# One load of the keys into two alternating tiles, and the local scores of two heads on row tiles of 64 rows

## The chip, the core and the metric

The kernel runs on one core of one Trainium2 chip. The metric is the device time of one execution in microseconds. Three runs of the kernel before took 741.83, 742.13 and 745.91 us, so its median is 742.13 us.

## What is computed

Three layers follow each other: an attention with a coarse and a local part, a bilinear feed-forward layer, and a mixture of eight experts with the best one chosen for each token. Cut to what matters:

```python
# q, k, v: (4, 8, 576, 64): batch, heads, positions, head size
q_d, k_d, v_d = means of q, k, v over groups of 4 positions
out_up = repeat(softmax(q_d @ k_d.T / 8) @ v_d, 4)
mask = abs(pos[:, None] - pos[None, :]) < 4
out_local = softmax(where(mask, q @ k.T / 8, -1e9)) @ v
x = out_up + out_local                      # (2304, 512)
x = ((x @ w1) * (x @ w2)) @ w3 @ w_out      # moe_ weights, float64
e = argmax(x @ w_gate); gate from softmax and a sigmoid of x @ w_output_gate
out = gate * relu(x @ w1[e]) @ w2[e]        # 8 experts
```

The first-layer weights come as float64 and are turned into float32 by bit operations on VectorE; each is then split into a high and a low part, and a product is three matmuls (`mm3`, L397 to L400).

## The kernel before

The work of the attention is cut into 16 units, each two heads of one batch (so 128 rows: 64 of head 0 above 64 of head 1). A unit goes through five steps: `a_T` (L176) sums groups of four positions of the queries (on POOL, into `qz`) and of the keys (on DVE, L185, from `kc` into `kd`); `a_S1` (L188) makes the local scores and the coarse scores and their exponentials; `a_S2` (L220) normalises and sums the values in groups of four; `a_V1` (L239) transposes the weights; `a_V2` (L256) multiplies by the values and writes the sum into `xr`. The list `side` (L286 to L293) puts them in order: in a round come a_V2 of unit u-4, a_V1 of u-3, a_S2 of u-2, a_S1 of u-1 and a_T of u, and `step` (L295) takes one or two entries off that list at points between the other work.

That other work is, in order: the gate products (L315), the product of `w3` and `w_out` (`w3_part`, `wc_half`, L345 to L363), the conversion of `w1` and `w2` (`w_part`, L367), then six groups of 384 tokens (`g1_step`, `g2_step`), routing, and the experts. The first group needs the attention of its tokens in `xr` (`x_split`, L382).

Local scores: a query block of 32 positions (24 of them new) needs 32 keys. Twenty-four blocks make twenty-four float32 matmuls at L196, each on a column strip of 32 columns of the array (`tile_position=(0, 32 * j)`). The two heads are held apart by `kz`, a tile with two copies in its free dimension: rows 0 to 63 of copy 0 hold head 0's keys, rows 64 to 127 of copy 1 hold head 1's, and the rest is zero. A matmul with 128 rows and 2 x 32 columns thus gives both heads' scores side by side in one PSUM bank, and one addition at L200 puts on the mask. A float32 matmul that is written once shows as two records with a load of weights each.

Loads go through SP's queue. The keys are read twice per unit: whole into `kc` (L157, one buffer, for the sums of four) and in two halves into `kz` (L164, one buffer). The queries go into two alternating tiles `qT0` and `qT1` (L158). `a_load(u + 1)` follows a_T of u; `a_loadk(u + 1)` and the load of the coarse values `a_loadd(u)` (tile `v4`, "v" in the profile, L168) follow a_S1 of u.

PSUM has eight banks: two each for `g1` and `g2`, one for the bit operations, and three in `psa` (tag `at`), taken in turn: a new tile waits for the readers of the tile three turns earlier. A unit takes one for the local scores, one for the coarse scores, two in a_V1 and two in a_V2. Routing takes some as well.

The order on each engine is written by a scheduler from priorities and its own estimate of times; `burst()` (L149) raises the priority of a group of matmuls. Each engine then runs its list in order.

Of the kernel before, what the change touches and what calls it, by code (L numbers as in the profile page):

```python
# [8 lines left out]
F32 = mybir.dt.float32  # L9
# [6 lines left out]
ALU = mybir.AluOpType  # L16
AX = mybir.AxisListType
# [3 lines left out]
P = 128  # L21
B, H, S, D = 4, 8, 576, 64
# [6 lines left out]
NU = B * H // 2  # L29
# [19 lines left out]
def attention_moe_kernel(ctx: ExitStack, tc: tile.TileContext, q, k, vw_in, v4_in, w1, w2, w3, w_out,  # L49
                         w_gate, w_ogate, e_w1, e_w2, out):  # L50
    nc = tc.nc
# [5 lines left out]
    psa = actx.enter_context(tc.tile_pool(name="psa", bufs=3, space=PSUM))  # L57
# [7 lines left out]
    def mt(shape, dt, name, tag=None, bufs=None):  # L65
        return main.tile(shape, dt, name=name, tag=tag or name, bufs=bufs)
# [4 lines left out]
    mask = mt([P, 6, 32], F32, "mask")  # L71
# [36 lines left out]
    def f64_load(m, n):  # L108
        if m == "o":
            t = mt([P, 512], I64, "f64w", tag=f"W{n}")  # L110
            src = w_out[P * n:P * n + P, :]
        elif m == "3":
            t = mt([P, 512], I64, "f64w", tag=f"W{8 + n % 4}")
            src = w3[n]
        else:
            t = mt([P, 512], I64, "f64", tag=f"W{3 + 4 * m}") if n % 2 and n < 6 else mt([P, 512], I64, "f64", bufs=2)
            src = (w1, w2)[m][n]
        for c in pieces(m, n):
            nc.sync.dma_start(out=t[:, c], in_=src[:, c])
        staged[m, n] = t  # L120
# [17 lines left out]
    def at(shape, dt, name, bufs=1):  # L138
        return att.tile(shape, dt, name=name, tag=name, bufs=bufs)

    kz = at([P, 2, 584], F32, "kz")
    qTs = [at([P, 584], F32, f"qT{i}") for i in range(2)]
    bd = at([P, 12, 96], F32, "bd")
    qz = at([P, 2, 144], F32, "qz")
    for t in (kz, *qTs, bd, qz):
        nc.gpsimd.memset(t, 0.0)
    st = {}

    def burst():  # L149

        return tc.high_priority(offset=600)

    def a_load(u):
        d = st.setdefault(u, {})
        qT = qTs[u % 2]
        kc = at([P, S], F32, "kc")
        nc.sync.dma_start(out=kc, in_=k[u])  # L157
        nc.sync.dma_start(out=qT[:, 0:S], in_=q[u])  # L158
        d.update(kc=kc, qT=qT)

    def a_loadk(u):
        for h in range(2):
            c = slice(64 * h, 64 * h + 64)
            nc.sync.dma_start(out=kz[c, h, 3:3 + S], in_=k[u, c])  # L164

    def a_loadd(u):
        v4 = at([72, 2, 4, 2 * D], F32, "v4")
        nc.sync.dma_start(out=v4.rearrange("p k r n -> p (k r n)"), in_=v4_in[u])  # L168
        st[u]["v4"] = v4

    def a_loadv(u):
        vw = at([P, 6, 2 * D], F32, "vw")
        nc.sync.dma_start(out=vw.rearrange("p c n -> p (c n)"), in_=vw_in[u])
        st[u]["vw"] = vw

    def a_T(u):  # L176
        d = st[u]
        qv = d["qT"][:, 0:S].rearrange("p (n r) -> p n r", r=4)
        hs = at([P, 144, 2], F32, "pt")
        nc.gpsimd.tensor_tensor(hs, qv[:, :, 0:2], qv[:, :, 2:4], op=ALU.add)  # L180
        for h in range(2):
            c = slice(64 * h, 64 * h + 64)
            nc.gpsimd.tensor_tensor(qz[c, h], hs[c, :, 0], hs[c, :, 1], op=ALU.add)
        dn = at([P, 144], F32, "kd")
        nc.vector.tensor_reduce(out=dn, in_=d["kc"].rearrange("p (n t) -> p n t", t=4), axis=AX.X, op=ALU.add)  # L185
        d["kd"] = dn

    def a_S1(u):  # L188
        d = st[u]
        qT = d["qT"]  # L190
        ps = psa.tile([P, 512], F32, name="at", tag="at")
        sl = ps[:, 0:384].rearrange("p (b h k) -> p b h k", b=6, h=2)
        with burst():
            for g in range(24):
                b, j = divmod(g, 4)
                nc.tensor.matmul(sl[32 * j:32 * j + 32, b], qT[:, 24 * g:24 * g + 32], kz[:, :, 24 * g:24 * g + 32],  # L196
                                 start=True, stop=True, tile_position=(0, 32 * j))
        sm = at([P, 6, 2, 32], F32, "sm", bufs=2)
        mx = at([P, 6, 2], F32, "mx")
        nc.vector.tensor_tensor(sm, sl, mask.unsqueeze(2).to_broadcast([P, 6, 2, 32]), op=ALU.add)  # L200
        nc.vector.tensor_reduce(out=mx, in_=sm, axis=AX.X, op=ALU.max)
        nc.gpsimd.tensor_tensor(sm, sm, mx.unsqueeze(3).to_broadcast([P, 6, 2, 32]), op=ALU.subtract)
        ps = psa.tile([P, 512], F32, name="at", tag="at")
        sd = ps[0:96, 0:432].rearrange("p (q k) -> p q k", q=3)
        qf = qz.rearrange("p h n -> p (h n)")
        with burst():
            for qb in range(3):
                nc.tensor.matmul(sd[:, qb], qf[:, 96 * qb:96 * qb + 96], d["kd"], start=True, stop=True)  # L208
        ed = at([96, 3, 144], F32, "ed", bufs=2)
        md = at([96, 3], F32, "md")  # L210
        nc.vector.tensor_reduce(out=md, in_=sd, axis=AX.X, op=ALU.max)
        nc.vector.tensor_scalar(md, md, -1.0 / 128, None, op0=ALU.mult)
        zd = at([96, 3], F32, "zd", bufs=2)
        nc.scalar.activation(out=sm, in_=sm, func=AF.Exp, scale=0.125)
        for qb in range(3):
            nc.scalar.activation(out=ed[:, qb], in_=sd[:, qb], func=AF.Exp, scale=1.0 / 128,
                                 bias=md[:, qb:qb + 1], accum_out=zd[:, qb:qb + 1])
        d.update(sm=sm, ed=ed, zd=zd)
# [69 lines left out]
    for b in range(B):  # L288
        for s in range(UB + 4):
            for lag, fn in ((4, a_V2), (3, a_V1), (2, a_S2), (1, a_S1), (0, a_T)):  # L290
                if 0 <= s - lag < UB:
                    side.append((fn, b * UB + s - lag))
    side.reverse()  # L293

    def step(n=1):  # L295
        for _ in range(n):
            if side:
                fn, u = side.pop()
                with tc.high_priority(offset=120):
                    fn(u)  # L300
                if fn is a_V1:
                    a_loadv(u)
                if fn is a_T and u + 1 < NU:
                    a_load(u + 1)
                if fn is a_S1:
                    if u + 1 < NU:
                        a_loadk(u + 1)
                    a_loadd(u)


# [578 lines left out]
    for n in range(4):  # L889
        f64_load("3", n)  # L890
        if n == 1:
            a_load(0)
            a_loadk(0)
    gps = ps2.tile([P, 512], F32, name="g2", tag="g2")
    for f in range(KF):
        gate_step(f, gps, staged.pop(("o", f)))
        step(GSTEP[f])
# [16 lines left out]
    for i in range(KF):  # L914
        if i == KF - 2:
            ahead()
        w3T[i] = [mt([P, KF, P], F32R, "w3T", tag=f"W{12 + 2 * (i % 2) + z}") for z in range(2)]
        for hf in range(2):
            n = 2 * i + hf
            w3_part(i, hf, w3T[i], staged.pop(("3", n)), wf3)  # L920
            if n + 4 < 2 * KF:
                f64_load("3", n + 4)
            step(W3STEP[i][hf])
        if i < KF - 2:
            order = ((i, 0), (i, 1))
        else:
            order = ((KF - 2, 0),) if i == KF - 2 else ((KF - 1, 0), (KF - 2, 1), (KF - 1, 1))
        for n, hf in order:
            wps[n, hf] = wc_half(n, hf, w3T[n])
            if (n, hf) == (KF - 1, 0):  # L930
                wc_out(KF - 2, 0, wps.pop((KF - 2, 0)))
            if (n, hf) != (KF - 2, 0):
                wc_out(n, hf, wps.pop((n, hf)))
        step(W3STEP[i][2])
# [171 lines left out]
```

## Time and profile before

| | |
|---|---|
| median of three runs | 742.13 us |
| profiled execution | 743.41 us, its span 741.7 us |
| TensorE busy | 706.0 us (95%), mean granted clock 0.986 |
| DVE, POOL, ACT busy | 437.9, 324.5, 280.3 us |
| DMA | 97.72 MB, mean 132 GB/s |

An engine's busy time is the time in which one of its instructions ran; TensorE's matmuls overlap, so a busy TensorE is not always a full one. The span is the time from the first to the last instruction of the profiled execution. A wait is put down to what came last before the waiting instruction. SPq is the queue of SyncE that issues loads.

### The profile page before, as it was taken

To read this page: it belongs to the slowest core of one execution; us is meant where nothing else is said; L and a number is where in the kernel's file an instruction comes from. 1 tells how busy PE (TensorE), PEld (TensorE's weight loads), DVE (VectorE), ACT (ScalarE), POOL (GpSimd) and SP (SyncE) were. 2 spreads that over 40 slices of the span, in tenths; PEclk is the share of its full clock that TensorE was granted. 3 is DMA by queue.
4 is the path that set the end of the run, shared out by engine and by line. 5 is a ranking of instruction groups with operands and counts; after the bars stand their busy time and mean duration, and the time that the engine had idled before them with its cause. 6 is when DMAs were issued, how large, how long until landed. Compare 5 with 4: busy or idle time off the path is not lost.

```text
span 741.7 us, 14714 instructions
## 1 busy us (share of the span) xinstructions
PE 706.0 (95%) x5710; PEld 671.9 (91%) x5711; DVE 437.9 (59%) x940; ACT 280.3 (38%) x624; POOL 324.5 (44%) x306
## 2 busy tenths in 40 slices
PE   5788999999999999999999999989999999999995
PEld 3677889989989998998999999979999999999994
DVE  8979899872565437254342342575756756766730
ACT  3436356541254135034212221244454444544610
POOL 6845586950263146123012020155564755854611
PEclk9899999999999999999999999989999999999999
DMA  8998657611153133110100100566444645545301
GB/s 326 316 243 246 186 142 246 212 57 57 28 161 111 43 92 96 57 45 24 57 30 1 43 0 30 171 224 219 170 154 149 218 166 203 184 162 221 115 24 40
DMA packets 38265, 97.72 MB, mean 132 GB/s; under 512 B 6019, under 2 KB 12931, under 8 KB 38193
## 3 DMA queue, kind: packets, MB, share of 16 engines
q1 hardware_dynamic: 34768, 86.82, 36.4%
q0 software_dynamic: 3424, 9.93, 3.7%
q8 instruction: 46, 0.75, 0.4%
q14 instruction: 27, 0.21, 0.1%
HBM read 84.93 MB, written 12.29 MB: 131 GB/s over the span
## 4 chain that ended last, share of the span: by engine, by line
PE 76%; DMA 7%; POOL 6%; issue 6%; DVE 4%; ACT 1%; SPq 0%; POOLq 0%; DVEq 0%; ACTq 0%
PE g L398 22%; PE g L399 21%; PE g L400 21%; DMA v<-in_v_dram 3%; PE at L268 2%; DMA vw<-in_vw_dram 2%; PE at L208 1%; PE at L196 1%; PE tr L694 1%; PE at L264 1%; PE tr L787 1%; PE g L330 1%; PE at L252 1%; POOL out_dram L777 1%; DMA early<-in_moe_w_dram 1%
## 5 line engine op out<-in xcount | busy, mean ns | idle before, releaser
L398 PE MATMUL g<-xh,W 128*128 128x384 f32 x384 | 131.0, 341 | 0.6 <-DVE a L427 0.5
L400 PE MATMUL g<-xh,W 128*128 128x384 f32 x384 | 129.8, 338 | 0.7 <-POOL W L377 0.6
L399 PE MATMUL g<-xl,W 128*128 128x384 f32 x384 | 129.3, 337 | 0.0
L721 DVE TENSOR_TENSOR W<-raw,W 128x1024 fp32r<-128x1024 f32 x32 | 87.9, 2781 | 32.6 <-ACT W L719 23.5
L721 POOL TENSOR_TENSOR W<-raw,W 128x1024 fp32r<-128x1024 f32 x29 | 82.9, 2880 | 36.9 <-ACT W L719 36.9
L398 PE MATMUL g<-xT,W 128*128 128x288 f32 (+6 forms) x256 | 82.0, 320 | 1.0 <-ACT xT L698 1.0
L431 POOL TENSOR_TENSOR h<-a,h 128x384 fp32r<-128x384 f32 x30 | 30.8, 1028 | 118.4 <-ACT h L429 118.4
L399 PE MATMUL g<-xT,W 128*128 128x288 f32 (+6 forms) x256 | 80.1, 313 | 0.0
L400 PE MATMUL g<-xT,W 128*128 128x288 f32 (+6 forms) x256 | 79.8, 312 | 0.0
L398 PEld LDWEIGHTS g<-xh,W 128*128 128x128 f32 x384 | 72.2, 188 | 2.1 <-DVE a L427 0.9
L400 PEld LDWEIGHTS g<-xh,W 128*128 128x128 f32 x384 | 72.1, 188 | 2.0 <-POOL W L377 1.8
L399 PEld LDWEIGHTS g<-xl,W 128*128 128x128 f32 x384 | 72.2, 188 | 0.3 <-issue 0.2
L398 PE MATMUL g<-h,W 128*128 128x288 f32 (+5 forms) x224 | 69.9, 312 | 0.0
L399 PE MATMUL g<-wc,h 128*128 128x272 f32 (+1 forms) x240 | 68.2, 285 | 0.0
L398 PE MATMUL g<-wc,h 128*128 128x272 f32 (+1 forms) x240 | 68.2, 285 | 0.0
L399 PE MATMUL g<-h,W 128*128 128x288 f32 (+5 forms) x224 | 68.0, 303 | 0.0
L400 PE MATMUL g<-h,W 128*128 128x288 f32 (+5 forms) x224 | 68.0, 303 | 0.0
L400 PE MATMUL g<-wc,h 128*128 128x272 f32 (+1 forms) x240 | 67.8, 285 | 0.0
L719 ACT CAST W<-raw 128x1024 fp32r<-128x1024 f32 x61 | 60.0, 1046 | 8.3 <-DMA raw<-in_moe_w_dram 4.4
L427 DVE TENSOR_TENSOR a<-g,a 128x384 f32<-128x384 f32 x48 | 26.6, 554 | 61.9 <-PE g L400 49.6
L747 ACT ACTIVATE h<-g 128x288 fp32r<-128x288 f32 (+6 forms) x64 | 27.9, 437 | 78.1 <-PE g L400 74.2
L777 POOL DMA_INDIRECT out_dram<-orow,b_si x24 | 23.5, 978 | 62.9 <-DVE orow L776 59.3
(255 smaller groups left out, 1716.3 us busy)
## 6 DMA issues: line engine op xcount, KB each, us to landing
raw<-in_moe_w_dram SPq DMA_DIRECT2D x61, 512.0 KB, 3.5
f64w<-in_moe_w_dram SPq DMA_DIRECT2D x16, 512.0 KB, 8.5
f<-in_moe_w_dram SPq DMA_DIRECT2D x16, 512.0 KB, 4.7
vw<-in_vw_dram SPq DMA_DIRECT2D x16, 384.0 KB, 4.9
kc<-in_k_dram SPq DMA_DIRECT2D x16, 288.0 KB, 8.8
qT<-in_q_dram SPq DMA_DIRECT2D x16, 288.0 KB, 3.2
kz<-in_k_dram SPq DMA_DIRECT2D x32, 144.0 KB, 4.1
v<-in_v_dram SPq DMA_DIRECT2D x16, 288.0 KB
```

Of the source, the lines that this page charges most:

```text
L196: nc.tensor.matmul(sl[32 * j:32 * j + 32, b], qT[:, 24 * g:24 * g + 32], kz[:, :, 24 * g:24 * g + 32], start=True, stop=True, tile_positio ...
L208: nc.tensor.matmul(sd[:, qb], qf[:, 96 * qb:96 * qb + 96], d["kd"], start=True, stop=True)
L268: nc.tensor.matmul(xl[c // 3][64 * h:64 * h + 64, 96 * (c % 3):96 * (c % 3) + 96], vw[:, c, D * h:D * h + D], bd[:, 2 * c + h, :], start=T ...
L398: nc.tensor.matmul(ps, whi, xhi, start=first, stop=False)
L399: nc.tensor.matmul(ps, whi, xlo, start=False, stop=False)
L400: return nc.tensor.matmul(ps, wlo, xhi, start=False, stop=last)
L427: nc.vector.tensor_tensor(a, pp[1][:, 0:G], a, op=ALU.mult)
L431: eng.tensor_tensor(lo, a, hi.bitcast(F32), op=ALU.subtract)
L719: nc.scalar.copy(out=hi, in_=t)
L721: ins = eng.tensor_tensor(lo, t, hi.bitcast(F32), op=ALU.subtract)
L747: return nc.scalar.activation(out=t[:, 0, 0:C], in_=ps[:, 0:C], func=AF.Relu), nc.vector.scalar_tensor_tensor(t[:, 1, 0:C], ps[:, 0:C], 0. ...
L777: ins = nc.gpsimd.indirect_dma_start(out=out, out_offset=bass.IndirectOffsetOnAxis(ap=rt["si"][0:n, r, b:b + 1], axis=0), in_=t[0:n], in_o ...
```

## The change

The two-copy tile `kz` and the single tile `kc` go. Two tiles `kT0` and `kT1` take the keys of both heads as they come, by one load per unit, three positions in; the sums of four read from the same tile. The local scores are made by 48 written matmuls in place of 24: each takes the 64 rows of one head only (a row tile of 64 rows in the column strip of 32), with 32 columns, and each head has a PSUM bank of its own. Two mask additions with 192 columns each take the place of the one with 384. `a_loadk` and its calls go.

```diff
-    kz = at([P, 2, 584], F32, "kz")
+    kTs = [at([P, 584], F32, f"kT{i}") for i in range(2)]
...
-        qT = qTs[u % 2]
-        kc = at([P, S], F32, "kc")
-        nc.sync.dma_start(out=kc, in_=k[u])
+        qT, kT = qTs[u % 2], kTs[u % 2]
+        nc.sync.dma_start(out=kT[:, 3:3 + S], in_=k[u])
         nc.sync.dma_start(out=qT[:, 0:S], in_=q[u])
...
-    def a_loadk(u):
-        for h in range(2):
-            c = slice(64 * h, 64 * h + 64)
-            nc.sync.dma_start(out=kz[c, h, 3:3 + S], in_=k[u, c])
...
-        nc.vector.tensor_reduce(out=dn, in_=d["kc"].rearrange("p (n t) -> p n t", t=4), axis=AX.X, op=ALU.add)
+        nc.vector.tensor_reduce(out=dn, in_=d["kT"][:, 3:3 + S].rearrange("p (n t) -> p n t", t=4), axis=AX.X, op=ALU.add)
...
-        ps = psa.tile([P, 512], F32, name="at", tag="at")
-        sl = ps[:, 0:384].rearrange("p (b h k) -> p b h k", b=6, h=2)
+        sl = [psa.tile([P, 512], F32, name="at", tag="at")[:, 0:192].rearrange("p (b k) -> p b k", b=6) for _ in range(2)]
         with burst():
             for g in range(24):
                 b, j = divmod(g, 4)
-                nc.tensor.matmul(sl[32 * j:32 * j + 32, b], qT[:, 24 * g:24 * g + 32], kz[:, :, 24 * g:24 * g + 32],
-                                 start=True, stop=True, tile_position=(0, 32 * j))
+                for h in range(2):
+                    c = slice(64 * h, 64 * h + 64)
+                    nc.tensor.matmul(sl[h][32 * j:32 * j + 32, b], qT[c, 24 * g:24 * g + 32], kT[c, 24 * g:24 * g + 32],
+                                     start=True, stop=True, tile_position=(64 * h, 32 * j))
...
-        nc.vector.tensor_tensor(sm, sl, mask.unsqueeze(2).to_broadcast([P, 6, 2, 32]), op=ALU.add)
+        for h in range(2):
+            nc.vector.tensor_tensor(sm[:, :, h], sl[h], mask, op=ALU.add)
...
-                    if u + 1 < NU:
-                        a_loadk(u + 1)
                     a_loadd(u)
```

## Rows read from the trace of the kernel before

**Rows 1.** Stretches: start:end, length, each engine's busy us (instructions), clock, DMA share, GB/s.
```profile
18.50:37.00 18.50, 13.87 (x134) 11.89 (x135) 17.11 (x43) 7.98 (x19) 14.88 (x21) 0.85 1.04 314
...
0.00:111.00 111.00, 90.25 (x1000) 77.82 (x1002) 97.93 (x216) 49.51 (x131) 72.21 (x100) 0.95 0.81 243
111.00:350.00 239.00, 236.82 (x2090) 223.36 (x2089) 135.02 (x362) 91.23 (x245) 100.27 (x114) 1.00 0.31 96
```
**Rows 2.** Waits of TensorE, 111 to 360 us: us in total, times, longest.
```profile
PE at L208 <- POOL qz L183: 0.9, 1, 0.9
```
**Rows 3.** Waits of DVE, 0 to 111 us.
```profile
DVE kd L185 <- DMA kc<-in_k_dram: 3.8, 2, 2.4
DVE sT L243 <- POOL sm L228: 2.6, 1, 2.6
```
**Rows 4.** Line of time of DVE: start us, us, what [idle before, releaser].
```profile
44.36 0.75 DVE L185 TENSOR_REDUCE kd<-kc 128x144 f32<-128x576 f32 x1 [1.43 <-DMA kc<-in_k_dram]
...
55.24 0.75 DVE L185 TENSOR_REDUCE kd<-kc 128x144 f32<-128x576 f32 x1 [2.38 <-DMA kc<-in_k_dram]
```
**Rows 5.** Line of time of SP's queue, 26 to 47 us.
```profile
26.64 0.33 SPq L158 DMA_DIRECT2D qT<-in_q_dram  x1
...
35.91 0.33 SPq L157 DMA_DIRECT2D kc<-in_k_dram  x1
...
40.74 1.11 SPq L164 DMA_DIRECT2D kz<-in_k_dram  x2
41.91 0.58 SPq L158 DMA_DIRECT2D qT<-in_q_dram  x1
...
46.08 0.33 SPq L157 DMA_DIRECT2D kc<-in_k_dram  x1
```
**Rows 6.** Waits of POOL, 0 to 111 us.
```profile
POOL v L235 <- DMA v<-in_v_dram: 18.6, 6, 5.3
```
**Rows 7.** Groups of instructions by form, DVE, 0 to 360 us: busy us, mean ns.
```profile
L200 DVE TENSOR_TENSOR sm<-at,mask 128x384 f32<-128x384 f32 x16 | 8.7, 541 | 0.2
...
L279 DVE TENSOR_TENSOR xr<-at,up 128x192 f32<-128x192 f32 x8 | 2.8, 346 | 0.0
```
**Rows 8.** Line of time of TensorE at unit 4's local scores.
```profile
86.00 0.88 PE L196 MATMUL at<-kz,qT 128*32 128x64 f32 x48
86.81 0.38 PE L400 MATMUL g<-wo,w3T 128*128 128x256 f32 x1
```
**Rows 9.** The tile `at` on TensorE: duration of one, ns, least/median/most.
```profile
L196 PE MATMUL at<-kz,qT x768: 216/219/317, 22.4 to 340.1; 128*32 128x64 f32 x192
...
L208 PE MATMUL at<-kd,qz x96: 283/286/447, 24.5 to 339.3; 128*96 128x144 f32 x96
```
**Rows 10.** Line of time of TensorE, coarse scores of unit 0.
```profile
24.96 0.65 PE L208 MATMUL at<-kd,qz 128*96 128x144 f32 x4
```
**Rows 11.** Stretch of 35 ns, L196 alone: TensorE (starts), weight loads (starts), clock, DMA.
```profile
116.43:116.47 0.04, 0.03 (x4) 0.03 (x4) 1.00 0.28 117
```
**Rows 12.** Lines of time of ACT, DVE and TensorE around unit 7's scores.
```profile
116.38 0.69 ACT L253 COPY pt<-at 72x288 f32<-72x288 f32 x2 [0.67 <-PE at L252]
...
120.44 0.54 DVE L200 TENSOR_TENSOR sm<-at,mask 128x384 f32<-128x384 f32 x1
...
116.44 0.86 PE L196 MATMUL at<-kz,qT 128*32 128x64 f32 x44
...
118.92 0.67 PE L268 MATMUL at<-bd,vw 128*64 128x96 f32 x12
...
122.35 0.72 PE L268 MATMUL at<-bd,vw 128*64 128x96 f32 x12
```
**Rows 13.** Line of time of TensorE at unit 8's scores.
```profile
198.24 0.31 PE L196 MATMUL at<-kz,qT 128*32 128x64 f32 x6
198.48 0.49 PE L208 MATMUL at<-kd,qz 128*96 128x144 f32 x2
...
200.88 0.40 PE L581 MATMUL at<-rb 128*128 128x288 f32 x1
```

More of the change, by code (lines that the diff above doesn't have):

```diff
@@ L144, in attention_moe_kernel @@
     qz = at([P, 2, 144], F32, "qz")
-    for t in (kz, *qTs, bd, qz):
+    for t in (*qTs, *kTs, bd, qz):
         nc.gpsimd.memset(t, 0.0)
@@ L154, in a_load @@
         d = st.setdefault(u, {})
-        qT = qTs[u % 2]
-        kc = at([P, S], F32, "kc")
-        nc.sync.dma_start(out=kc, in_=k[u])
+        qT, kT = qTs[u % 2], kTs[u % 2]
+        nc.sync.dma_start(out=kT[:, 3:3 + S], in_=k[u])
         nc.sync.dma_start(out=qT[:, 0:S], in_=q[u])
-        d.update(kc=kc, qT=qT)
-    def a_loadk(u):
-        for h in range(2):
-            c = slice(64 * h, 64 * h + 64)
-            nc.sync.dma_start(out=kz[c, h, 3:3 + S], in_=k[u, c])
+        d.update(kT=kT, qT=qT)
     def a_loadd(u):
@@ L189, in a_S1 @@
         d = st[u]
-        qT = d["qT"]
-        ps = psa.tile([P, 512], F32, name="at", tag="at")
-        sl = ps[:, 0:384].rearrange("p (b h k) -> p b h k", b=6, h=2)
+        qT, kT = d["qT"], d["kT"]
+        sl = [psa.tile([P, 512], F32, name="at", tag="at")[:, 0:192].rearrange("p (b k) -> p b k", b=6) for _ in range(2)]
         with burst():
@@ L892, in attention_moe_kernel @@
             a_load(0)
-            a_loadk(0)
     gps = ps2.tile([P, 512], F32, name="g2", tag="g2")
```

## The prediction

> **What bounds the kernel now.** I read the stretches first, then who waits in each. From 111 to 350 us TensorE is busy 236.8 of 239 us at clock 1.00, while DVE has 135 and the DMA engines 0.31 [rows 1]; its waits there are of three kinds, the largest of them 0.9 us [rows 2]. So in that stretch every nanosecond of TensorE counts one for one. From 0 to 111 us it is another machine: TensorE has 90 of 111 us, DVE 98, and between 18 and 37 us the DMA engines read 1.04, that is full [rows 1]. The prologue (the float64 conversions, the product of w3 and w_out, and seven units' local scores) ends when DVE has done its list, so what counts there is DVE's work and DVE's idle time. The largest idle item is the reduction of the keys (L185) waiting for its load: 3.8 us in two waits; the next is 2.6 us [rows 3]. Both waits are seen on DVE's line of time, 1.43 us before 44.36 and 2.38 us before 55.24 [rows 4].
>
> **Loads.** The change removes 32 transfers of 144 KB (two a unit) and puts the one load of the keys, 288 KB, into two alternating tiles. What that is worth is read on SP's queue: the queries of unit 2 were asked for at 26.64, its keys only at 35.91, since the single kc tile had first to be reduced for unit 1; the queries of unit 3 at 41.91, its keys at 46.08 [rows 5]. The queries already alternate, and the new key tile has the same kind of wait: the readers of unit u-1, whose local scores come before a_T(u) in the order of steps. So the keys go out beside the queries, 9.3 and 4.2 us earlier; a landing took about 8.4 us (35.91 to 44.36) and 9.2 us (46.08 to 55.24) [rows 4, 5], so unit 2's keys land at about 35 and unit 3's at about 51, both before DVE's wait begins (42.9 and 52.9). Both waits go: **-3.8 us**. The bound on the other side is 0, if DVE finds another wait in that place. Late next is the value load: POOL stood 18.6 us in the prologue waiting for it [rows 6], and it reaches DVE only through the 2.6 us item. Queued behind the new load on SP are the queries, the weights and the values, as behind the old; the pair of kz issues held SP for 1.11 us a unit [rows 5], and that goes. Five pairs fall before 75 us, 1.5 MB; at the 314 GB/s of that stretch [rows 1] this is 4.7 us of a full DMA system. DVE's next wait is for POOL, not for a DMA [rows 3], so I take 0 and keep -4.7 as the bound. The first load now follows the memset of its tile, done on POOL long before the weights on SP let that load go: nothing.
>
> **DVE.** One mask addition over 384 columns (541 ns) becomes two of 192, each priced as L279 with 128x192, also out of PSUM: 346 ns [rows 7]. That is 2 x 346 - 541 = 151 ns a unit, **+1.1 us** for the seven units of the prologue. The nine later ones lie under TensorE; without that cover they cost +1.4. The reduction reads the same 576 columns, three further in: nothing.
>
> **TensorE.** Twenty-four products are written now, 48 records with a load of weights each; one unit's burst starts at 86.00 and the next work at 86.81, so 0.81 us [rows 8]. Its 48 starts lie within 0.88 - 0.22 = 0.66 us [rows 8, 9]; the four column strips run side by side, so that is 12 rounds of 55 ns, 0.86 ns for each of 64 columns. L208, on the whole array, agrees: (0.65 - 0.29)/3 = 0.121 us for 144 columns, 0.84 [rows 9, 10]. After the change there are 96 records with 32 columns on eight tiles (two row tiles, four strips). No row shows row tiles. Lower bound of the time: all eight run together, 12 rounds of about 29 ns, 0.35 us. Then the pace of starting matters: in 35 ns four pairs of load and matmul started [rows 11], the first at 116.44, so at most 8 ns a pair; 96 pairs at 8 ns are 0.77 us. Upper bound: nothing faster than the mean pace of today's burst, 0.66/48 = 14 ns, which is 1.32 us. A unit thus costs -0.31, +0.11 or +0.66 us. I take the first, because the four strips already run fully side by side and a strip's two row tiles write to different banks. In the bound stretch nine units (7 to 15) count: **-2.8 us**, with ends of -2.8 and +5.9. In the prologue TensorE is no bound: 0.
>
> A start every 14 ns on average [rows 8, 9] is faster than a rule of the Trainium skill allows (TensorE: Matmul & The Clock Gate, "Wait — 56ns, not 53.3ns?": start to start never falls below about 25 ns, however few columns). By that rule, as an estimate, 96 starts would take 2.4 us and the nine units would cost about +16 us; this trace contradicts it for work spread over strips.
>
> **PSUM.** The pool `psa` has three banks and each unit now takes seven turns of it instead of six; the local scores and the coarse scores of one unit need all three. A turn waits for the reader three turns back. The second head's bank now waits for the first copy of V1's transposes (before, only the coarse scores did), and the next V2 waits with its first bank for the mask addition (before, with its second). Behind a waiting matmul stands the whole of TensorE's order. For unit 7 the copies begin at 116.38 while the scores begin at 116.44 and a copy takes 0.35 [rows 12]: about 0.4 us. Five late units (7, 10, 11, 14, 15) come right after a V1, so 0 to 2.0; I take the middle, **+1.0 us**.
>
> **Sum.** The profiled execution took 743.4 us, 1.3 over the median of the runs shown, 742.1. 743.4 - 3.8 + 1.1 - 2.8 + 1.0 = 738.9, and 1.3 less for the median: **737.6**.
>
> **The rivals.**
> *The starts hold the burst at 8 ns.* For it: a pair of load and matmul has never been seen closer. Against: both run on tiles that were idle. -2.8 becomes +1.0: 741.4.
> *The prologue keeps its length.* The keys come early, but DVE then waits for the values' chain (POOL's 18.6 us). -3.8 becomes 0: 741.4.
> *Twice the matmuls at today's mean pace, 14 ns*, because row tiles of one strip take turns or starts cost more. -2.8 becomes +5.9: 746.3. The whole turns slower than before where a pair takes more than about 9 ns (0.66 us plus a ninth of the 1.7 that the rest gains, over 96). The eight starts in 35 ns speak against it.
> *The bank ring stalls TensorE (the slower side).* At unit 7, V2's first bank started at 118.92 and its second only at 122.35, after the mask addition that began at 120.44 and takes 0.54 [rows 12]. If now the first also waits to 120.98 and nothing is placed between, 2.1 us are lost at each of the five units: +10.5 in place of +1.0, 747.1. It decides from 1.1 us a unit on. Against: the scheduler put other matmuls between, and can again.
> *The bursts are torn.* At unit 8 the scores and the coarse scores alternate and take 198.24 to 200.88, 2.64 us [rows 13], where 0.81 and about 0.9 in one piece would do (six records of 0.121, and 0.15 for the change of shape, as 0.81 is over 0.66). Units 8, 9 and 15 look so. That the heads stand side by side then isn't true: if all nine are torn, 6 x 0.9 = +5.4: 743.0. If none is, -2.7.
>
> **How the numbers follow.** Forecast 0.44, pace of 8 ns 0.15, prologue keeps its length 0.15, pace of 14 ns 0.10, ring 0.10, torn 0.06. About 0.5% (3.7 us) is what a measurement of this kernel tells from no change, so faster means below 738.4 and slower above 745.8. Of the forecast nearly all lies below 738.4 (0.40), of the two at 741.4 a fifth (0.06): faster 0.46. The slower cases give 0.14 (the 14 ns pace lies on the line), the rest is 0.40. The low end takes the forecast, the DMA bytes in part and whole bursts (737.6 - 3.4 - 2.7), 731.5; the high end stops short of the two slower rivals, 745.5.
>
> **What would show it.** DVE has no wait for the keys in the prologue, and TensorE's full stretch begins about 3 us earlier; if not, the loads' step is wrong. The burst's 96 records span about 0.35 us and the next work starts 0.5 us after the first; 0.77 or 1.3 names the pace. The mask additions last 346 ns each. Waits of TensorE's local-score lines for ACT's copies or DVE's additions between 111 and 350 us, above 1 us in all, mean the ring. Most of all the prediction fails if the order that the scheduler writes differs elsewhere: a later x_split or more torn bursts would cover all these terms.

## The result: slower by 6.7 us, and the profile after

The changed kernel took 748.89 us (median), the kernel before 742.18 us in the same series: a ratio of 1.0075, 95% interval 1.0058 to 1.0092. The forecast of 737.6 us and its range, which ended at 745.5, were missed on the other side. The profiled execution took 750.43 us, its span 748.7 us (743.41 and 741.7 before).

Stretches of the changed kernel (start:end, length, busy us and instructions of PE, PEld, DVE, ACT, POOL, clock, DMA share, GB/s):

```profile
18.50:37.00 18.50, 15.81 (x285) 12.64 (x284) 16.63 (x32) 7.38 (x19) 13.82 (x19) 1.00 1.00 344
37.00:55.00 18.00, 14.16 (x185) 12.08 (x185) 15.76 (x47) 6.70 (x24) 11.88 (x16) 0.72 0.56 173
0.00:111.00 111.00, 90.83 (x1308) 77.94 (x1310) 101.52 (x220) 49.71 (x136) 68.66 (x98) 0.94 0.68 223
111.00:350.00 239.00, 233.93 (x2489) 222.47 (x2488) 141.80 (x368) 86.97 (x231) 101.12 (x114) 1.00 0.27 84
```

The kernel before, 37 to 55 us:

```profile
37.00:55.00 18.00, 15.70 (x198) 13.18 (x198) 14.02 (x32) 7.24 (x21) 8.20 (x9) 0.96 0.94 246
```

Set beside [rows 1], the loads did what they should: the DMA share of 37 to 55 us fell from 0.94 to 0.56, and by 111 us DVE had idled 9.5 us instead of 13.1. But DVE was busy 3.6 us more and got no further: it ran 220 instructions by then, 216 before, and 7 of the 220 are second mask additions. The additions account for 1.1 us; the rest is that the same instructions took longer. The eight subtractions of w3 on DVE, before and after (0 to 111 us; busy us, mean ns):

```profile
L351 DVE TENSOR_TENSOR w3T<-wf,w3T 128x512 fp32r<-128x512 f32 x8 | 7.6, 948 | 0.0
```

```profile
L346 DVE TENSOR_TENSOR w3T<-wf,w3T 128x512 fp32r<-128x512 f32 x8 | 10.1, 1257 | 0.2 <-ACT w3T L344 0.2
```

TensorE's clock in 37 to 55 us was 0.72, where it was 0.96; but the kernel before had its slow stretch sooner (0.85 in 18.5 to 37 us [rows 1], now 1.00), and over 0 to 111 us the clock is 0.94 against 0.95. The first matmul of the first group (`xh`) starts at 111.7 us instead of 105.2, the last of that group at 171.2 instead of 163.0, and from 365 us on everything is 6.6 to 7.2 us late. So the loss arises in the prologue and in the first group.

The keys on SP's queue in the changed kernel, for units 2 and 3, and the largest waits of DVE from 0 to 111 us (waited for: us in total, times, longest):

```profile
26.56 0.33 SPq L156 DMA_DIRECT2D kT<-in_k_dram  x1
...
33.87 0.33 SPq L156 DMA_DIRECT2D kT<-in_k_dram  x1
```

```profile
DVE md L208 <- PE at L205: 2.2, 1, 2.2
DVE xr L276 <- ACT up L268: 1.5, 2, 1.3
DVE su L222 <- ACT sm L211: 1.4, 1, 1.4
```

The keys are asked for 9.4 and 12.2 us sooner than in [rows 5]. The wait of [rows 3] for them is gone from DVE's list; other waits, for TensorE and ACT, stand there now.

What TensorE did from 29 to 44 us is read on its line of time (start us, us, what, [idle before, releaser]):

```profile
29.70 1.13 PE L192 MATMUL at<-kT,qT 64*32 64x32 f32 x72
30.76 0.98 PE L205 MATMUL at<-kd,qz 128*96 128x144 f32 x6
31.66 0.33 PE L192 MATMUL at<-kT,qT 64*32 64x32 f32 x24
31.92 1.06 PE L325 MATMUL g<-wot,wg 128*32 128x128 f32 x8
...
35.37 0.38 PE L333 MATMUL g<-ident,gs 128*128 128x128 f32 x2
36.96 0.70 PE L249 MATMUL at<-ident,ed 96*72 96x96 f32 x6 [1.09 <-DVE sm L197]
...
39.82 0.86 PE L192 MATMUL at<-kT,qT 64*32 64x32 f32 x48 [2.02 <-ACT ed L213]
...
41.78 0.59 PE L393 MATMUL g<-wo,w3T 128*128 128x272 f32 x1 [1.09 <-DVE wo L337]
42.92 0.59 PE L394 MATMUL g<-wo,w3T 128*128 128x272 f32 x1 [0.55 <-DVE wo L338]
43.31 0.43 PE L395 MATMUL g<-wo,w3T 128*128 128x272 f32 x1
```

Unit 1's keys were there early, so the scheduler put its scores (29.70) ahead of the last gate products (31.92) and of the gate's transposes (35.37). In the kernel before they came at 37.79, behind the gate's transposes at 28.36. Half of the w3 product multiplies by the gate's columns, which DVE copies out of those transposes. The eight copies, before and after (duration ns, first and last start us):

```profile
L342 DVE CAST wo<-g x8: 153/158/175, 28.8 to 37.7; 128x16 fp32r<-128x16 f32 x8
```

```profile
L337 DVE CAST wo<-g x8: 133/158/163, 41.6 to 54.2; 128x16 fp32r<-128x16 f32 x8
```

They come 13 to 16 us later, though the transposes come only 7.0 us later: DVE's list has conversions and attention steps ahead of the first copy. TensorE waits for the copies at 41.78 and 42.92. Two other waits in that line are of the bank ring: V1's transposes at 36.96 for a mask addition, unit 2's scores at 39.82 for ACT to have read a bank of coarse scores. From 38.4 to 48.6 us TensorE runs at a granted clock of 0.50, the lower of its two levels (1.2 of 2.4 GHz): a matmul with 272 columns takes 0.43 us at 43.31 (0.59 right behind a wait), where it takes 0.29 at the full clock. The kernel before has such a stretch too, from 31.6 to 38.4 us. How far the w3 product has come by 80 us (its matmuls alone: length, busy us and count, clock, DMA share, GB/s), before and after:

```profile
0.00:80.00 80.00, 28.73 (x182) 0.94 0.88 269
```

```profile
0.00:80.00 80.00, 27.25 (x158) 0.91 0.76 252
```

Up to the first matmul on `xh`, and from there to the end of the first group, before and after:

```profile
0.00:105.20 105.20, 84.71 (x941) 72.84 (x942) 92.13 (x201) 46.20 (x123) 66.41 (x94) 0.95 0.82 247
105.20:163.00 57.80, 56.29 (x473) 51.76 (x470) 49.28 (x99) 30.91 (x76) 46.06 (x47) 1.00 0.58 184
```

```profile
0.00:111.70 111.70, 91.53 (x1314) 78.64 (x1316) 102.22 (x221) 50.41 (x137) 69.36 (x98) 0.94 0.68 222
111.70:171.20 59.50, 54.45 (x482) 49.73 (x481) 48.40 (x87) 26.49 (x62) 43.46 (x44) 1.00 0.50 154
```

In the prologue TensorE thus idled no longer than before (20.2 us, 20.5 before). It lost 1.7 us more to the half clock there, and the local and coarse scores of units 0 to 6 held it 16.1 us instead of 13.3. The idle time that is new lies in the first group: 5.1 us instead of 1.5. The weights that this group multiplies by are converted 4.6 us later at the first (ACT's L371 at 108.2, 103.6 before) and 8.1 us later at the sixteenth (167.4, 159.3). The largest wait for them, with what it goes back to on DVE and POOL:

```profile
113.42 2.62 DVE L226 TENSOR_SCALAR zd<-zd 96x3 f32<-96x3 f32 x1
...
114.06 1.96 POOL L387 TENSOR_TENSOR xl<-xr,xh 128x384 fp32r<-128x384 f32 x2
...
115.96 0.67 DVE L129 SCALAR_TENSOR_TENSOR wf<-f,cv 128x512 uint32<-128x512 uint32 x1
...
116.66 0.62 ACT L371 CAST W<-wf 128x512 fp32r<-128x512 f32 x1 [3.54 <-DVE wf L129]
...
117.33 0.44 PE L393 MATMUL g<-xh,W 128*128 128x384 f32 x1 [2.18 <-ACT W L371]
```

The scaling of `zd` has 3 columns and took 0.17 us at the median before. Here it took 2.62 and ended 0.03 us after POOL's subtraction, and the conversion stood behind it.

### The profile page after: what moved, and what is told of

Same layout as the page of the kernel before. It is cut to its first block, busy times and chain, and to the rows that moved or that the text cites. A ratio compares the mean times of both kernels' runs of the same rounds, so it can differ in the third digit from the quotient of the medians.

```text
span 748.7 us, 16209 instructions
## 1 busy us (share of the span) xinstructions
PE 710.3 (95%) x6478; PEld 676.7 (90%) x6479; DVE 449.8 (60%) x956; ACT 279.5 (37%) x624; POOL 325.4 (43%) x307
## 4 chain that ended last, share of the span: by engine, by line
PE 77%; DVE 8%; issue 5%; POOL 4%; DMA 4%; ACT 1%; SPq 0%; POOLq 0%; DVEq 0%; ACTq 0%
PE g L393 22%; PE g L395 22%; PE g L394 22%; PE at L192 2%; PE at L205 2%; PE at L265 2%; DMA v<-in_v_dram 1%; PE tr L689 1%; PE at L261 1%; PE tr L782 1%; POOL W L372 1%; DVE cv L127 1%; PE g L325 1%; DMA early<-in_moe_w_dram 1%; DVE wf L129 1%
```

## The experiments

Theory A: the scheduler used the early keys to put attention ahead of the gate's finishing, and this place costs TensorE. Theory B: the row tiles themselves cost (twice the matmuls, seven turns in three banks, two additions). Theory C: every new order is a throw of the dice. The numbers are medians of five rounds; in brackets the ratio to the kernel before on the same chip (742.1 to 743.4 us) and its interval.

**Holding the early attention steps.** In the changed kernel, the steps of the first two rounds of w3 may follow only behind the gate's last transpose and last copy.

```diff
-            step(W3STEP[i][hf])
+            if i < 2:
+                with tc.issue_after(held[0]), tc.issue_after(held[1]):
+                    step(W3STEP[i][hf])
```

> The changed kernel with one thing put back: the first four attention steps that are traced after gate_finish (sums of unit 1, scores of unit 1 and so on) are queued on TensorE and DVE behind gate_finish's last transpose and its last copy. Loads, row tiles, banks and additions stay as in the changed kernel. Theory A (the keys come early, so the scheduler puts unit 1's scores and sums ahead of the finishing of the gate, and the product of w3 and w_out starts late): the w3 product is back within 1 us of the kernel before at its tenth part (42.8 us) and the time falls by 5 to 7 us, to 742 to 744. Theory B (row tiles: twice the matmuls, three banks a unit, two additions): the time stays within 2 us of the changed kernel's 748.9. Theory C (a lottery of the order, nothing in particular): anything between 742 and 750, with the loss in another stretch.

744.99 us, 1.0028 (1.0008 to 1.0048). That is 3.9 us under the changed kernel, where A had expected 5 to 7. By 80 us the w3 product had 240 matmuls done, where the changed kernel had 158 and the kernel before 182. From its tenth part on, its matmuls came 3 to 14 us earlier than in the kernel before. So the place of those steps does cost TensorE, as A says. The lead over the kernel before was all given back further on, line of TensorE and a stretch:

```profile
108.69 0.25 PE L192 MATMUL at<-kT,qT 64*32 64x32 f32 x4 [1.07 <-ACT pt L250]
...
111.35 0.74 PE L261 MATMUL at<-pt,vd 72*64 72x144 f32 x2 [0.72 <-DVE sm L197]
```

```profile
111.00:125.00 14.00, 13.65 (x84) 10.76 (x85) 8.17 (x20) 6.70 (x20) 8.26 (x10) 0.63 0.37 111
```

Two ring waits, then V2 and the scores by turns of two, and 14 us at a clock of 0.63.

**Row tiles alone, out of `kz`, with the loads of before.**

```diff
+                for h in range(2):
+                    c = slice(64 * h, 64 * h + 64)
+                    nc.tensor.matmul(sl[h][32 * j:32 * j + 32, b], qT[c, 24 * g:24 * g + 32], kz[c, h, 24 * g:24 * g + 32],
+                                     start=True, stop=True, tile_position=(64 * h, 32 * j))
```

> The kernel before with the row tiles alone: 48 written matmuls of 64 rows out of kz, a bank for each head, two mask additions; kc, kz and their loads as before. Theory A: the keys of unit 1 still come late, its scores stay behind the gate, and the time is within 2 us of before (741 to 744), with about 0.15 us more for each burst. Theory B: 747 to 750. Theory C: anything between.

747.27 us, 1.0075 (1.0046 to 1.0104). This is B's range: unit 1's scores (37.2 us) stand behind the gate's transposes (30.6) here, and the kernel is slower by 5.1 us all the same.

**A single key tile.** This kernel reads other data: the keys of unit u+1 are loaded before unit u's local scores are written, so those scores use the next unit's keys. It serves for its order alone.

```diff
-    kTs = [at([P, 584], F32, f"kT{i}") for i in range(2)]
+    kTs = [at([P, 584], F32, "kT0")]
```

> The changed kernel with one key tile in place of two: one load a unit, row tiles and banks as in the change, but a load must wait until the unit before has used the tile. Theory A: the keys are late again, the gate is finished before any scores of unit 0, the time is 741 to 745. Theory B: 747 to 750.

738.22 us, 0.9944 (0.9922 to 0.9967). Here every score waits for the following keys, and the gate is finished before any score. A later start of the attention was faster than both kernels.

**Early sums alone**: the kernel before with two alternating `kc` and the loads of `kz` as they were.

```diff
+    kcs = [at([P, S], F32, f"kc{i}") for i in range(2)]
...
-        kc = at([P, S], F32, "kc")
+        kc = kcs[u % 2]
```

> The kernel before with two alternating tiles kc for the sums of the keys, nothing else: this is the loads' term of the prediction by itself. Both of DVE's waits for the keys (3.8 us) should go. The prediction's step: 3.8 us less, 738 to 739. Theory A: the scores still wait for kz, so the gate stays ahead of unit 1's scores; DVE's waits go, but other work of DVE or TensorE is late next, 740 to 743. Theory B: 740 to 743.

749.67 us, 1.0093 (1.0062 to 1.0123). DVE's waits for keys are gone, unit 1's scores (38.8 us) stay behind the gate's transposes (28.7), and the kernel is slower by 7.5 us, outside the ranges of A and B. Both halves lose; B and C can't be told apart by them.

**Nearly the same order of scores with and without the change.** On TensorE the scores of units 1 to 6 are held behind the matmuls of the w3 product (counted as written) behind which they stood, or nearly stood, before. In both kernels the attention steps are also taken off `side` sooner (`W3STEP`; in the second table of holds `GSTEP` too). The second table of holds starts later, as the single tile did: {0: 31, 1: 72, 2: 119, 3: 184, 4: 312, 5: 368}.

```diff
-W3STEP = ((1, 1, 0), (1, 1, 0), (1, 1, 0), (1, 1, 0), (1, 1, 1), (1, 1, 1), (1, 1, 0), (1, 1, 0))
+W3STEP = ((1, 1, 1), (1, 1, 1), (1, 1, 1), (1, 1, 1), (1, 1, 1), (1, 0, 0), (1, 0, 0), (1, 0, 0))
+HOLD = {1: 25, 2: 72, 3: 112, 4: 224, 5: 261, 6: 324}
...
+                    if fn is a_S1 and u in HOLD:
+                        hold.enter_context(tc.issue_after(mml[HOLD[u] - 1]))
```

> The kernel before with a hold on TensorE only: the local and coarse scores of units 1 to 6 may not start before the 25th, 72nd, 112th, 224th, 261st and 324th matmul of the w3 product, the places that they have (or nearly have) in the kernel before. It is the control of the next run. Theory A (the place of the early scores against the gate's finishing decides): about the time of before, 740 to 745 us. Theory B (the row tiles cost, whatever the order): the same. Theory C (every new order is a throw of the dice): anything from 736 to 750.

> The changed kernel with the same hold as the run before it: unit 1's scores come after the gate's finishing again. Theory A: the loss of 6.8 us goes; the difference to the held kernel before is the sum of the small terms only (loads -3.8 to 0, additions +1.1, bursts at 8 ns a pair +0.1 a unit, ring 0 to 2), so -2 to +3 us, some 740 to 745. Theory B (twice the matmuls, three banks, two additions): +5 to +7 against the held kernel before, as row tiles alone gave +5.1, so 747 to 750. Theory C: no fixed relation to the run before it.

> The kernel before with later scores: unit 0's first scores after the 31st matmul of the w3 product (so behind the gate's finishing), those of units 1 to 5 after the 72nd, 119th, 184th, 312th and 368th: the order that the single key tile fell into (738.2 us). Theory A: finishing the gate first lets TensorE work earlier on the w3 product; faster than before by 2 to 6 us, 736 to 740. Theory B says nothing of it and keeps 742. Theory C: 736 to 750.

> The changed kernel with the later scores of the run before it. Theory A: faster than the changed kernel by 9 to 14 us and within -2 to +3 us of the held kernel before, 735 to 742. Theory B: 5 to 7 us over the run before it whatever that is. Theory C: no fixed relation.

| holds | before | changed | the change is worth |
|---|---|---|---|
| none | 742.18 | 748.89 | +6.7 |
| old places | 748.67 (1.0070, 1.0046 to 1.0093) | 738.79 (0.9955, 0.9932 to 0.9977) | -9.9 |
| later | 752.01 (1.0113, 1.0082 to 1.0144) | 739.10 (0.9947, 0.9924 to 0.9969) | -12.9 |

B falls as it stood: in two of three orders the changed kernel is the faster one, and in both it beats the kernel before without holds by 0.5%. A holds for the changed kernel: with unit 1's scores behind the gate again, and the other units held too, it gains 10.1 us. It doesn't hold as a rule, since a later start made the kernel before slower. And the control missed its expectation of 740 to 745 us: in the kernel before, the holds left the scores of units 1 to 3 behind the same 25, 72 and 112 matmuls and those of units 4 to 6 behind 12 more each, and it lost 6.5 us. So -9.9 and -12.9 compare two held kernels, of which the one before suffers from the holds; C is not refuted. Nor do the scores stand behind the same matmuls in both kernels of the first pair: those of units 1 to 4 start behind 25, 72, 112 and 224 in the kernel before and behind 15, 67, 126 and 248 in the changed one. Stretches 28 to 80 us of the changed kernel with the scores at their old places:

```profile
28.00:55.00 27.00, 23.76 (x359) 19.90 (x357) 26.63 (x73) 12.15 (x40) 18.86 (x24) 1.00 0.71 240
55.00:80.00 25.00, 25.00 (x320) 23.08 (x318) 22.79 (x48) 15.20 (x40) 12.03 (x12) 1.00 0.75 235
```

and of the kernel before with the same holds:

```profile
28.00:55.00 27.00, 20.81 (x208) 17.66 (x208) 22.88 (x60) 10.23 (x30) 14.78 (x18) 0.81 0.96 268
55.00:80.00 25.00, 22.60 (x252) 20.87 (x249) 20.09 (x45) 13.47 (x41) 15.17 (x18) 0.93 0.72 212
```

In the first DVE is idle for 0.4 of 27 us and TensorE's clock doesn't fall; in the second DVE idles 4.1 us with the DMA engines at 0.96, and the clock falls three times by 80 us. By 111 us DVE had run 235 instructions in the first, 206 in the second. This is the gain that the forecast hoped for; in the changed kernel without holds, with 220, it isn't there.

**Whole bursts.** One hold, the coarse scores of a unit behind its last local score on TensorE, keeps the two from alternating.

```diff
-        with burst():
+        with burst(), tc.issue_after(loc.ins):
             for qb in range(3):
                 nc.tensor.matmul(sd[:, qb], qf[:, 96 * qb:96 * qb + 96], d["kd"], start=True, stop=True)
```

> The kernel before, with one hold: the coarse scores of a unit come after its last local score on TensorE, so that the two no longer alternate. Theory T (torn bursts cost what the change of shape costs): local and coarse scores of 16 units took 17.1 + 15.1 us of TensorE's time before; whole they would take 16 x (0.81 + 0.9) = 27.4, so -2 to -5 us, 737 to 740. Theory A (the place of the early scores and TensorE's clock in the prologue decide): unit 0 and 1 stay where they were, so 742 with what T gives in the full stretch only, 739 to 742.

> The changed kernel with the same hold; unit 1's scores still stand ahead of the gate's finishing. Theory A: the loss of 6.8 us before 111 us stays, with a gain of 2 to 4 us from the full stretch: 745 to 748. Theory T (the loss of the change is its torn bursts): 741 to 743.

> The changed kernel with unit 1 to 6's scores held at their old places (738.8 us) and whole bursts besides. Theory T: local and coarse scores took 20.4 + 15.9 us in that run, whole about 27 to 30, so -3 to -8 us: 731 to 736. Theory A: no tearing counts where TensorE waits anyway; nine late units in the full stretch give -1 to -3: 736 to 738.

> The changed kernel with the later scores (739.1 us) and whole bursts. Theory T: -3 to -8 us, 731 to 736. Theory A: -1 to -3, 736 to 738. Either way under the kernel before.

Before 737.77 (0.9923, 0.9894 to 0.9953), changed 749.57 (1.0094, 1.0058 to 1.0129), changed with old places 748.97 (1.0066, 1.0036 to 1.0095), changed with later places 740.85 (0.9968, 0.9946 to 0.9990). Theory T (torn bursts cost) holds for the kernel before and fails for the changed one: its scores took 5.4 us less of TensorE in the third run than torn (table below), and it lost 10.2. The line of TensorE in that run shows one reason:

```profile
37.88 0.29 PE L400 MATMUL g<-wo,w3T 128*128 128x272 f32 x1
42.26 1.15 PE L250 MATMUL at<-ident,ed 96*72 96x96 f32 x6 [4.09 <-DVE sm L198]
...
46.43 0.43 PE L400 MATMUL g<-wo,w3T 128*128 128x272 f32 x1
```

Unit 0's transposes need the bank of unit 1's first local scores, three turns back; the mask addition that frees it stands on DVE behind the eight gate copies and several conversions, at 41.77. TensorE waits 4.1 us, and its clock is at the lower level from 40.8 to 47.6 us.

**The same, with unit 1's additions placed sooner on DVE.**

```diff
+            with tc.issue_after(add[1]) if n >= 3 else ExitStack():
                 w3_part(i, hf, w3T[i], staged.pop(("3", n)), wf3)
```

> The changed kernel with held scores and whole bursts (749.0 us), and one hold on DVE: the conversions of w3 from the fourth half on come after unit 1's two mask additions. In that run TensorE stood 4.1 us before V1's first transposes of unit 0, waiting for those additions (three turns back in the ring of banks), and ran at half clock for the 6 us behind it. Theory R (the ring of three banks with seven turns, and the clock that falls after such a wait): the additions come about 3.7 us sooner, the wait falls under 1 us, TensorE's clock in 38 to 48 us is above 0.9, and the w3 product is 4 to 7 us earlier at its 30% than in that run. Total 740 to 745. Theory L (no single wait decides): the wait goes, the total stays at 747 to 751.

744.95 us, 1.0020 (0.9997 to 1.0043). TensorE's line:

```profile
39.11 0.70 PE L250 MATMUL at<-ident,ed 96*72 96x96 f32 x6 [0.95 <-POOL w3T L352]
...
45.48 0.58 PE L399 MATMUL g<-wo,w3T 128*128 128x256 f32 x1 [3.24 <-DVE wc L364]
```

The ring wait went and 4.0 of the 10.2 us came back. A wait for another DVE step took its place and the clock fell all the same, from 44.8 to 51.6 us. Theory R (the ring and the clock behind it) just meets its range of 740 to 745 us, but not its clock above 0.9: 0.84 in 38 to 48 us.

**The halves under the old places, and the kernel before with whole bursts and the later start.** The edits are those above, put together.

> The kernel before with two tiles kc (early sums; 749.7 us in its own order), scores held as in the pair 748.7 (before, held) and 738.8 (changed, held). Theory K (of the 9.9 us between that pair the early keys bring the larger part): 739 to 743. Theory W (the row tiles with their two banks bring it): 747 to 750. Theory L: neither alone, anything.

> The kernel before with row tiles out of kz (747.3 us in its own order), scores held as in that pair. Theory K: 747 to 750, with the loads of before. Theory W: 739 to 743. Theory L: anything.

> The kernel before with the later scores (752.0 us) and whole bursts (737.8 with whole bursts alone). Unit by unit, local and coarse scores took 20.9 + 15.9 us of TensorE in the run with later scores and 13.7 + 13.0 in the one with whole bursts: Theory T (tearing is what the later scores cost the kernel before): 752 - 10 = 742 or less, 736 to 742. Theory R: half clock or a wait for the ring or for the values takes part of that back: 742 to 749.

751.36 (1.0102, 1.0076 to 1.0128), 756.01 (1.0152, 1.0120 to 1.0184) and 741.62 us (0.9971, 0.9947 to 0.9995). Against the held kernel before, 748.67, the halves are worth +2.7 and +7.3, together they are worth -9.9. Theories K and W (one half brings the larger part) both fall; T holds for the third run. One reason is on SP's queue of the run with early sums, with TensorE's wait from 27 to 130 us:

```profile
42.26 1.11 SPq L166 DMA_DIRECT2D kz<-in_k_dram  x2
45.36 0.33 SPq L159 DMA_DIRECT2D kc<-in_k_dram  x1
54.63 1.83 SPq L166 DMA_DIRECT2D kz<-in_k_dram  x2
```

```profile
PE at L198 <- DMA kz<-in_k_dram: 1.8, 1, 1.8
```

In the kernel before that wait was 1.0 us. The single `kz` can't be loaded before the last unit's scores are made (40.74 before, [rows 5]; 42.26 here): with early sums alone the scores are as late as ever. Either half also keeps all the bytes, and the DMA share of 28 to 55 us is 1.00 and 0.93 in them, 0.71 with the whole change. That the bytes explain the rest was not tried.

**Whole bursts in units 7 to 15 only**: the prologue keeps its order to the instruction.

```diff
-        with burst(), tc.issue_after(loc.ins):
+        with burst(), (tc.issue_after(loc.ins) if u >= 7 else ExitStack()):
```

> The changed kernel with held scores (738.8 us), whole bursts for units 7 to 15 alone: TensorE's order up to unit 7 is that of the held run, to the instruction. Theory F (tearing costs only in the stretch where TensorE is full, and filling TensorE's gaps in the prologue keeps its clock): the gain of whole bursts without the loss, 738.8 - 2 to 5 us: 734 to 737, with no half clock before 111 us. Theory L: the end moves by some us either way, 734 to 745.

> The kernel before with whole bursts for units 7 to 15 alone; its prologue's order is unchanged. Theory F: the change of shapes saved in the full stretch, of which units 8, 9 and 15 alternate most: 2 to 5 us, 737 to 740; against the run beside it, a unit's local scores in one piece give the pace of row tiles: 0.95 us against 0.81, so +1.3 us for nine units. Theory L: 737 to 748.

741.77 us (0.9987, 0.9963 to 1.0011; 738.79 with torn bursts) and 740.03 us (0.9960, 0.9936 to 0.9984; 742.97 for the kernel before). Tearing in the full stretch thus costs the kernel before 2.9 us. In the changed kernel the scores took 3.8 us less, but TensorE idled 3.7 us more, 1.4 of them before ACT's `a` (L428, 2.4 us against 1.0), and two stretches of half clock (155.4 to 158.8 and 274.8 to 278.2 us) cost 3.4. Theory F (whole late bursts gain without a loss) is half right.

These two runs time a burst in one piece at the full clock. Unit 10 of the kernel before, then of the changed one, then a changed unit's second half:

```profile
214.94 0.88 PE L196 MATMUL at<-kz,qT 128*32 128x64 f32 x48
215.74 0.98 PE L208 MATMUL at<-kd,qz 128*96 128x144 f32 x6
```

```profile
213.09 1.02 PE L193 MATMUL at<-kT,qT 64*32 64x32 f32 x96
214.05 0.98 PE L206 MATMUL at<-kd,qz 128*96 128x144 f32 x6
...
118.14 0.62 PE L193 MATMUL at<-kT,qT 64*32 64x32 f32 x48
118.70 0.98 PE L206 MATMUL at<-kd,qz 128*96 128x144 f32 x6
```

From start to the next work's start: 0.80 us on strips, 0.96 on row tiles, 0.56 for half a unit. So 48 records more cost 0.40 us, 8.3 ns a pair of load and matmul, and 0.16 us is fixed.

**One sum for all runs.** Three items of the trace, each up to the 600th matmul on `xh` (399.9 us before): TensorE's idle time; the time lost at half clock (stretches of 2 us, each 2 x (1 - clock)); and the time that local and coarse scores held TensorE (from each start to the next, less idle time). They are read from the profiled execution, the median from all.

| kernel | median | idle | half clock | scores | sum |
|---|---|---|---|---|---|
| before | 742.2 | 22.9 | 5.1 | 32.3 | 60.3 |
| changed | 748.9 | 25.2 | 6.8 | 34.7 | 66.7 |
| changed, old places | 738.8 | 17.0 | 0.0 | 36.3 | 53.3 |
| changed, later | 739.1 | 13.9 | 1.7 | 35.9 | 51.5 |
| changed, old places, whole | 749.0 | 29.8 | 8.5 | 30.9 | 69.2 |
| before, old places | 748.7 | 24.8 | 6.8 | 35.2 | 66.8 |
| before, later | 752.0 | 19.9 | 1.7 | 36.8 | 58.4 |
| before, whole | 737.8 | 23.8 | 5.1 | 26.7 | 55.6 |
| row tiles, old places | 756.0 | 24.3 | 11.9 | 37.8 | 74.0 |

For the changed kernel against before: +2.3, +1.7 and +2.4 make 6.4 of the 6.7 us (idle: 0.3 less in the prologue, 3.5 more in the first group, 0.9 less behind it). The median less the sum is 678 to 688 us in every run but one: before with the later start has 694, with V2 and the scores by turns from 70 to 75.5 us (V2 took about 3 us more of TensorE; the rest is open). The sum says where time went, not what sent it there.

## Why the prediction was wrong

- **Loads, -3.8: the waits right, what follows from them wrong.** Keys were asked for 9 to 12 us earlier, both waits went, and DVE idled 3.6 us less by 111 us. The step that failed is the one that let DVE's idle time count one for one and set TensorE in the prologue at 0. DVE turned none of it into progress: the new additions took 1.1 us of it, other instructions took longer, and the weights of the first group came 4.6 to 8.1 us later. TensorE lost 1.7 us to the clock and 2.8 to the scores of units 0 to 6 in the prologue, and it idled 3.5 us more in the first group. The order that the scheduler wrote is new as well: unit 1's scores went ahead of the gate. The last sentence of the prediction named this ("if the order that the scheduler writes differs elsewhere") and gave it no chance and no price; it was the case.
- **The late next.** It was put as the value load. In the changed kernel DVE's largest waits were for TensorE and ACT (2.2 and 1.5 us); with early sums alone, TensorE waited for the load of `kz` (1.8 to 2.0 us, 1.0 before).
- **DVE, +1.1: right.** The additions took what was forecast from [rows 7], by form from 0 to 360 us (busy us, mean ns, idle before):

```profile
L197 DVE TENSOR_TENSOR sm<-at,mask 128x192 f32<-128x192 f32 x32 | 10.3, 344 | 0.1
```

- **TensorE, -2.8: wrong sign.** A unit costs +0.16 us in one piece and 2 x 0.56 - 0.80 = +0.3 in two, against -0.31; the rival of 8 ns a pair, +0.11, was nearly exact. Nine units make +1.4 to +2.9 where both kernels have bursts of that kind. In the changed kernel itself the local scores of units 7 to 15 took 10.4 us, 10.2 before, since the kernel before tore its own; so the term came out at +0.2 instead of -2.8. I should have taken the pace that [rows 11] showed. The Trainium skill (TensorEngine Tiling (Array Packing), Instruction Overhead) warns of this: the tiling factor isn't to be taken from a dimension that is already small, since a matmul has an overhead that doesn't shrink. The trace agrees: 64 columns became 32, and the burst went from 0.80 to 0.96 us.
- **PSUM ring, +1.0: right in kind, in the wrong place.** After 111 us TensorE waited once for a bank, 0.5 us, where 0 to 2.0 was allowed. Before 111 us, where I had put nothing, it waited 2.0, 1.1 and 0.9 us, and in another order 4.1. The Trainium skill (TensorEngine Tiling (Array Packing), Gotcha 1: PSUM Pressure) says that row tiling raises the pressure on PSUM. The trace agrees: the kernel before waited 0.2 us for a bank there.
- **Torn bursts: the mechanism right, the units wrong.** Units 8, 9 and 15 were torn before [rows 13]. In the changed kernel local scores held TensorE 19.7 us in all, 17.1 before, but the difference lies in units 0 to 6 (9.3 and 6.9 us), which the rival left out. Whole late bursts were reckoned at -2.7 for the kernel before and gave -2.9; that is partly luck, since the scores took 4.5 us less there and 1.5 us of idle time came back.

Shown is that the change is worth +6.7, -9.9 or -12.9 us under three orders, and where the time sits: half clock, the scores of the prologue, and waits for late weights in the first group. That the early scores of unit 1 are the cause is shown in part: holding them with three more steps brought back 3.9 us, holding all six units 10.1. Not shown is why DVE's instructions took longer in the changed kernel, why the holds cost the kernel before 6.5 us though they moved its scores little, and why the two halves add to +10 when alone and to -9.9 together. No order was found from a rule: the later start helped the changed kernel and hurt the one before. The fastest kernel run, before with whole bursts (737.8), doesn't need the change; the changed kernel with scores at their old places (738.8) is as fast within the intervals.

## What to carry over

Where a scheduler writes the order, a transfer that comes early moves work as well as ending a wait: before pricing it, ask which instructions will now be ready first, and hold them where they stood if other engines wait for what they overtake. Price a split of a small matmul by the pace of starts that the trace shows. A ring of PSUM banks ties TensorE to the place of its reader in another engine's list, and in these runs a wait there cost the wait and often a stretch of half clock with it. An engine's busy time is not its progress: count what it has done by a given time.

## What the runs showed of the hardware

Row tiles of 64 rows with 32 columns ran at 8.3 ns a pair of load and matmul: 96 pairs on eight tiles took 0.96 us where 48 pairs with twice the columns on four strips took 0.80 (0.81 in [rows 8]). Twice the tiles at half the columns bought nothing. In the changed kernel the granted clock fell to 0.50 at 38.4 us, inside the wait of 2.0 us that began at 37.80 and behind one of 1.1 us; it stayed there until 48.6 us, although TensorE was busy 7.0 of those 10.2 us. DVE's short scalings of `zd` and `su` took over 0.4 us 15 times in the changed kernel and 4 times before, at the longest 2.62 us where the median before was 0.17; each of these 19 ended 0.02 to 0.10 us after an instruction of POOL. That POOL held them up fits this and was not tried.
